# Order of the weight conversions in the opening of an FFT-and-MLP kernel: a skew of one piece, fold sums copied later, conversions moved ahead of the main loop

## The chip, the cores and the metric

One core of a Trainium2 chip. The metric is the device time of one execution in microseconds (us).

## The reference, cut to what matters

```python
x = 8 x 3008 x 256                                 # float32
X = real(fft(fft(x, axis=1), axis=2))              # over 3008 = 47 * 64, then over 256
h = X.reshape(24064, 256) @ w_in                   # 256 -> 2048, weights in float64
g = h * clip(h + 3, 0, 6) / 6
out = g @ w_out                                    # 2048 -> 256
```

## The kernel before

The main loop runs 4 x 12 x 8 steps: `mlp1` makes two half products u and v on TensorE, VectorE and ScalarE make the gated a, GpSimd adds up c, and `mlp2` accumulates seven products (acc). One step of it keeps TensorE busy for 4.75 us, and nothing else limits it. The *opening* must come first: stage 1 of the FFT for the first pair of batches (eight chunks, each a fold of x on VectorE and then matmuls), the conversion of 16 pieces of float64 weights to float32, the folding of w_in with the DFT matrix, and stage 2 of the first group.

A piece passes through three engines. `exponent_a` is two ScalarE instructions, `exponent_b` two matmuls, `exponent_c` one ScalarE instruction in place, `mantissa` two VectorE instructions, and `join` multiplies the two halves. After each second piece `use_pair` folds (w_in, on TensorE, with ScalarE copying the sums) or mixes (w_out, four VectorE instructions). Programs of the engines run in the order in which they are written.

```python
    ps_h = ctx.enter_context(tc.tile_pool(name="ps_h", bufs=3, space=PSUM))   # the three "uv" banks
    # ...
    def exponent_a(j):                                                       # ScalarE
        top = raw[j][:].bitcast(I16).rearrange("p (n four) -> p n four", four=4)[:, :, 3]
        for i in range(2):
            low = PM[:, j % 2, i].bitcast(U8).rearrange("p (n two) -> p n two", two=2)[:, :, 0]
            nc.scalar.activation(low, top, AF.Identity, bias=bias[:, i:i + 1], scale=(1 - 2 * i) / 16.0)

    def exponent_b(j):                                                       # TensorE, takes a uv bank
        ex = ps_h.tile([P, WB], F32, tag="uv", name="ex")
        for i in range(2):
            nc.tensor.matmul(ex[:], E[:, i], PM[:, j % 2, i].bitcast(F16), start=(i == 0), stop=(i == 1))
        exs[j] = ex

    def exponent_c(j):                                                       # ScalarE
        nc.scalar.activation(exs[j][:].bitcast(I32), exs[j][:], AF.Identity, scale=2.0 ** 23)
    # ... mantissa(j): two VectorE instructions; join(j): frac * ex on VectorE, frees the uv bank

    def fold_w_in(n):
        # ...
        for blk in range(2):
            ps = bank([P, WB], "wps")
            for i in range(2):
                nc.tensor.matmul(ps[:], C[:, i, blk * P:(blk + 1) * P], ws[i], start=(i == 0), stop=(i == 1))
            nc.scalar.copy(W1[:, blk, cs], ps[:])                            # at once
    # ...
    for c in range(NXC):                                                     # the eight chunks of stage 1
        if c + 2 < NXC:
            load_x(first, c + 2)
        load_w(c + 2)
        exponent_a(c)
        on_pe = c not in (2, 4, NXC - 1)          # fold_first: 3 VectorE instructions, more matmuls
        # ... fold of chunk c on VectorE
        if c > 0:
            join(c - 1)
        mantissa(c)
        for i in range(XC // 2):
            (stage1_first if on_pe else stage1)(first, c, i)
        exponent_b(c)
        exponent_c(c)
        if c in (2, 4, 6):
            use_pair(c // 2 - 1)
        # ...
    for j in range(NXC, 14):                                                 # the tail: pieces 8 to 13
        # ... load_w(j + 2)
        exponent_a(j)
        exponent_b(j)
        if j > NXC:
            exponent_c(j - 1)
        join(j - 1)
        mantissa(j)
        if j % 2 == 0:
            use_pair(j // 2 - 1)
    # ... last c, join and use_pair, then keep_awake(4)
    for i in range(2):
        stage2(first, 0, i)
    spread(first, 0)
    # ... pieces 14 and 15 are put behind steps 0 and 1 of the main loop
    mlp1(*chunk(0))                                                          # the fill of the main loop
    mlp1(*chunk(1))
    combine(*chunk(0))
```

`mlp1` takes two uv banks, u and v. `keep_awake(n)` issues n matmuls of zeros, meant to keep TensorE's clock up.

Of the kernel before, what the change touches and what calls it, by code (L numbers as in the profile page):

```python
# [56 lines left out]
def kernel(  # L57
# [171 lines left out]
    def evict_z(pr, c, i, ps):  # L229
        if i == 0:  # L230
            pr.z[c] = zpool.tile([PZ, XC, D], F32, tag="z", name="z")
            if c == 0:
                pr.zd = dpool.tile([2, NK1, 2, NS, D], F32, tag="zd", name="zd")
                pr.zq = dpool.tile([2, NK1, 2, NS], F32, tag="zq", name="zq")
# [13 lines left out]
    def turn_column(pr, c, z):  # L248
        n = XC if c < NXC - 1 else XC - 1
        zc = zpool.tile([PZ, XC], F32, tag="zc", name="zc")  # L250
        nc.scalar.activation(zc[:, 0:n], z[:, 0:n, P], AF.Identity, scale=F[0:PZ, 5 * PZ + NP * NXC:])
        to = pr.zq[:, :, :, c * XC:(c + 1) * XC].rearrange("b k c n -> c (b k) n")
        for ci in range(2):
            nc.sync.dma_start(out=to[1 - ci, :, 0:n], in_=zc[ci::2, 0:n])
        if n < XC:
            for ci in range(2):
                nc.sync.dma_start(out=to[ci, :, n], in_=z[ci::2, n, P])


    def load_g(pr, gr):  # L260
        g = gpool.tile([P, 2 * KK, D + 1], F32, tag="g", name="g")
        ks = slice(gr * 2 * KK, (gr + 1) * 2 * KK)
        for b in range(2):
            gb = g[b * N2:(b + 1) * N2]
            nc.sync.dma_start(out=gb[:, :, 0:D], in_=pr.zd[b].rearrange("k c n d -> (c n) k d")[:, ks, :])
            nc.sync.dma_start(out=gb[:, :, D], in_=pr.zq[b].rearrange("k c n -> (c n) k")[:, ks])
# [246 lines left out]
    def fold_w_in(n):  # L513

        cs = slice(n * WB, (n + 1) * WB)
        ws = [w.pop(("in", n, i)) for i in range(2)]
        for blk in range(2):
# [3 lines left out]
            nc.scalar.copy(W1[:, blk, cs], ps[:])  # L521
        nc.sync.dma_start(out=wn[n:n + 1], in_=W1[P - 1:P, 1, cs])
# [20 lines left out]
    nc.sync.dma_start(out=F[:], in_=c_stage1)  # L543
    nc.vector.tensor_copy(IX[:], F[:, 5 * PZ:5 * PZ + NP * NXC])
# [5 lines left out]
    load_t(0)  # L550

    load_forward(first, 0)
    load_forward(first, 1)
    load_partners(first, 0)
    load_w(0)
    load_partners(first, 1)
    load_w(1)

    bias = wpool.tile([P, 2], F32, tag="bias", name="bias")
    for i in range(2):  # L560
        nc.vector.memset(bias[:, i:i + 1], (2 * i - 1) * 7.5 / 16.0 - 896.0)
    nc.vector.memset(half[:], 0.5)
    PM = wpool.tile([P, 2, 2, WB], I16, tag="PM", name="PM")
    nc.vector.memset(PM[:], 0x6400)
    E = wpool.tile([P, 2, P], F16, tag="E", name="E")
    nc.scalar.copy(E[:], CE[:])
    for b in range(2):
        nc.vector.memset(T[(1 - b) * N2:(2 - b) * N2, b], 0.0)
    wn = dpool.tile([NWI, WB], F32, tag="wn", bufs=1, name="wn")

    for c in range(NXC):
# [3 lines left out]
        exponent_a(c)  # L575
        on_pe = c not in (2, 4, NXC - 1)
        if on_pe:
# [4 lines left out]
        if c > 0:  # L582
            join(c - 1)
        mantissa(c)
        for i in range(XC // 2):
            (stage1_first if on_pe else stage1)(first, c, i)
        exponent_b(c)
        exponent_c(c)
        if c in (2, 4, 6):
            use_pair(c // 2 - 1)  # L590
        if c in (3, 5):
            load_wn(PIECES[c - 3][1])
    load_g(first, 0)
    load_g(first, 1)
    load_t(1)
    for j in range(NXC, 14):
        if j + 2 < 16:
            load_w(j + 2)
        exponent_a(j)
        exponent_b(j)  # L600
        if j > NXC:
            exponent_c(j - 1)
        join(j - 1)
        mantissa(j)
        if j % 2 == 0:
            use_pair(j // 2 - 1)
    exponent_c(13)
    join(13)
    use_pair(6)
    load_wn(PIECES[6][1])  # L610
    load_wn(PIECES[8][1])
    keep_awake(4)
# [11 lines left out]
    def beside(p):  # L624
# [6 lines left out]
        if p == 0:  # L631
            for t, fs in enumerate([[(f, 14) for f in (exponent_a, exponent_b, mantissa)],
# [143 lines left out]
```

## Time and profile before

| | before |
|---|---|
| median of the first 3 runs | 2009.54 us (2009.37 to 2010.34) |
| profiled execution | 2007.46 us, span 2005.7 us |
| TensorE busy | 1962.5 us of the span |
| first matmul of acc | 95.78 us from the start |
| acc of the fifth step | 119.58 us |
| from there to the end | 1886.1 us |

The last row is the reason for looking at the opening alone. TensorE is full from the fifth step to its end, so a change of the opening is worth what it moves the acc of the fifth step.

ScalarE in the tail, from its timeline (columns: start, length, engine, line, operation with out<-in, and in brackets the idle time in front with what ended it):

```profile
62.40 0.59 ACT L521 COPY W<-wps 128x512 f32<-128x512 f32 x1 [2.18 <-PE wps L520]
64.12 0.58 ACT L521 COPY W<-wps 128x512 f32<-128x512 f32 x1 [1.13 <-PE wps L520]
...
71.50 0.58 ACT L521 COPY W<-wps 128x512 f32<-128x512 f32 x1 [3.21 <-PE wps L520]
```

The copies of the fold sums stand in ScalarE's order at the place where the fold's matmuls are only being issued, so ScalarE idles 2.18 and 1.13 us for one fold and 3.21 us ahead of the other's first copy, while the next pieces need it. The second is TensorE in the fill of the main loop:

```profile
91.15 1.10 PE L324 MATMUL v<-q,W 127*128 127x256 f32 x4 [1.64 <-DVE a L356]
...
94.84 1.10 PE L324 MATMUL v<-q,W 127*128 127x256 f32 x4 [1.72 <-DVE a L356]
95.78 0.60 PE L378 MATMUL acc<-a,G 128*128 128x256 f32 x2
```

With three uv banks, the v of the second and of the third step each wait for a bank: two holes of 1.64 and 1.72 us. Between them 2 us of matmuls run, and they run at full clock, 1.10 us for four of 256 columns.

### The profile page before, as it was taken

The page shows a single profiled execution, that of the slowest core. Times are in us where ns is not written, and L with a number is a line of the kernel's source. Part 1 is how long each engine was busy: PE and PEld are TensorE (multiplying, and loading weights), DVE is VectorE, ACT ScalarE, POOL GpSimd, SP SyncE. Part 2 cuts the span into 40 slices and gives each one's busy share as a digit, 9 for nine tenths or more (in the row PEclk, how much of TensorE's full clock was granted, in tenths as well). Part 3 has the DMA queues.
Part 4 walks back from the last instruction along what each step waited for, and adds up shares of the span by engine and source line. Part 5 has one row for each costly group of instructions (what it writes and reads, how often), then busy time and mean ns, then how long its engine had stood idle before and what let it go on. Part 6 is the DMA issues. An engine that isn't in the chain of part 4 may idle for free.

```text
span 2005.7 us, 28349 instructions
## 1 busy us (share of the span) xinstructions
PE 1962.5 (98%) x9144; PEld 1686.7 (84%) x9144; DVE 1444.6 (72%) x2707; ACT 694.7 (35%) x1196; POOL 1419.3 (71%) x1612
## 2 busy tenths in 40 slices
PE   8799999999999999999999999999999999999997
PEld 4388888888888888888888888888888888888886
DVE  6677767776777676777777777777678777777775
ACT  5433333333333333333333333333333333333322
POOL 3277778786677787777658877778666667667665
PEclk8899999999999999999999999999999999999999
DMA  9502211111111122210111221112110101101100
GB/s 294 143 21 56 59 39 47 49 47 35 27 35 50 40 49 53 54 51 25 41 26 29 67 55 42 51 43 52 35 27 19 27 17 26 33 12 27 27 12 19
DMA packets 159560, 93.52 MB, mean 47 GB/s; under 512 B 131595, under 2 KB 144395, under 8 KB 159414
## 3 DMA queue, kind: packets, MB, share of 16 engines
q1 hardware_dynamic: 149942, 58.23, 11.6%
q0 software_dynamic: 9472, 33.49, 6.0%
q8 instruction: 74, 1.21, 0.3%
q14 instruction: 72, 0.59, 0.1%
HBM read 54.32 MB, written 37.33 MB: 46 GB/s over the span
## 4 chain that ended last, share of the span: by engine, by line
PE 92%; DVE 3%; ACT 1%; issue 1%; POOL 0%; SPq 0%; DMA 0%; DVEq 0%; POOLq 0%; ACTq 0%
PE acc L378 55%; PE v L324 16%; PE u L324 16%; PE ps L279 2%; PE ps L226 2%; DVE a L356 1%; ACT t L353 1%; DVE u L337 1%; DVE s L329 1%; PE wps L520 0%; ACT PM L456 0%; DVE o L404 0%; DVE v L343 0%; PE awake L537 0%; PE ps L223 0%
## 5 line engine op out<-in xcount | busy, mean ns | idle before, releaser
L368 POOL TENSOR_TENSOR c<-a 128x512 f32<-128x512 f32 (+1 forms) x384 | 478.9, 1247 | 446.4 <-PE acc L378 361.3
L378 PE MATMUL acc<-c,G 128*128 128x256 f32 (+1 forms) x3072 | 712.1, 375 | 0.0
L353 ACT ACTIVATE t<-u,half 128x512 f32<-128x512 f32 (+2 forms) x416 | 272.3, 654 | 1101.1 <-DVE u L337 1089.5
L378 PEld LDWEIGHTS acc<-c,G 128*128 128x128 f32 x3072 | 577.5, 190 | 72.7
L329 DVE SCALAR_TENSOR_TENSOR s<-qn,WN,u 128x256 f32<-128x256 f32 x768 | 334.5, 477 | 351.6 <-PE u L324 348.8
L378 PE MATMUL acc<-a,G 128*128 128x256 f32 (+1 forms) x2304 | 550.6, 374 | 0.0
L378 PEld LDWEIGHTS acc<-a,G 128*128 128x128 f32 x2304 | 433.8, 190 | 57.4
L324 PE MATMUL v<-q,W 127*128 127x256 f32 x1536 | 397.0, 380 | 8.0 <-DVE a L356 8.0
L324 PE MATMUL u<-q,W 128*128 128x256 f32 x1536 | 394.3, 379 | 0.0
L324 PEld LDWEIGHTS v<-q,W 127*128 127x128 f32 x1536 | 289.5, 190 | 55.7 <-PE u L324 8.4
L324 PEld LDWEIGHTS u<-q,W 128*128 128x128 f32 x1536 | 287.3, 190 | 57.8 <-issue 13.9
L356 DVE SCALAR_TENSOR_TENSOR a<-t,u 128x512 f32<-128x512 f32 (+2 forms) x416 | 266.2, 646 | 95.2 <-ACT t L353 90.5
L368 POOL TENSOR_TENSOR c<-c,a 128x256 f32<-128x256 f32 (+1 forms) x384 | 275.2, 717 | 30.1
L368 POOL TENSOR_TENSOR c<-a,c 128x256 f32<-128x256 f32 (+1 forms) x384 | 275.0, 716 | 30.1
L337 DVE TENSOR_TENSOR u<-s,v 128x512 f32<-128x512 f32 (+1 forms) x384 | 263.0, 685 | 41.1 <-DVE s L329 1.4
L353 ACT ACTIVATE t<-v,half 128x512 f32<-128x512 f32 (+1 forms) x384 | 257.0, 669 | 5.8 <-DVE v L343 4.3
L343 DVE TENSOR_TENSOR v<-v,s 128x512 f32<-128x512 f32 (+1 forms) x384 | 257.7, 671 | 1.1
L356 DVE SCALAR_TENSOR_TENSOR a<-t,v 128x512 f32<-128x512 f32 (+1 forms) x416 | 255.2, 620 | 0.4 <-ACT t L353 0.2
L368 POOL TENSOR_TENSOR r<-w,e 128x256 f32<-128x256 f32 (+1 forms) x96 | 92.2, 981 | 3.8
L384 ACT ACTIVATE e<-acc 128x512 f32<-128x512 f32 (+1 forms) x192 | 86.9, 542 | 2.9 <-PE acc L378 2.8
L404 DVE STREAM_TRANSPOSE o<-r 128x256 f32<-128x256 f32 (+1 forms) x192 | 72.4, 414 | 6.4 <-POOL r L368 6.4
L236 ACT COPY z<-ps 96x512 f32<-96x512 f32 x64 | 36.9, 581 | 82.4 <-PE ps L226 64.1
(81 smaller groups left out, 750.2 us busy)
## 6 DMA issues: line engine op xcount, KB each, us to landing
out_dram<-o SPq DMA_DIRECT2D x736, 32.0 KB
zd<-z SPq DMA_DIRECT2D x32, 384.0 KB
g<-zd SPq DMA_DIRECT2D x48, 256.0 KB
xt<-in_x_dram POOLq DMA_DIRECT2D x21, 384.0 KB, 3.8
qn<-qd SPq DMA_DIRECT2D x23, 256.0 KB
st<-in_moe_w_in_dram POOLq DMA_DIRECT2D x8, 512.0 KB, 9.6
st<-in_moe_w_out_dram POOLq DMA_DIRECT2D x8, 512.0 KB, 5.2
xt<-in_x_dram POOLq DMA_DIRECT2D x7, 376.0 KB, 3.9
```

The lines of the kernel that those rows point to most:

```text
L226: nc.tensor.matmul(ps[0:PZ], F[0:PR, 0:PZ], y[:, 2 * i:2 * i + 2, :], start=True, stop=True)
L279: nc.tensor.matmul(ps[:, blk, 2 * u:2 * u + 2], g[:, kk, blk * (P + 1):blk * (P + 1) + P], T[:, :, gr, blk, kk], start=True, stop=True)
L324: nc.tensor.matmul(ps[:, i], W1[r, blk, f * P:(f + 1) * P], q[r, blk, of:of + KC], start=True, stop=True)
L329: nc.vector.scalar_tensor_tensor(s[:, i].rearrange("p k n -> p (k n)"), qn[:, of * N2:(of + KC) * N2], WN[:, f:f + 1], u[:, i].rearrange(" ...
L337: nc.vector.tensor_tensor(u[:, :, 0:ns], s[:, :, 0:ns], v[:, :, 0:ns], op=AL.add)
L343: nc.vector.tensor_tensor(v[:, :, 0:nm], v[:, :, 0:nm], s[:, :, 0:nm], op=AL.subtract)
L353: nc.scalar.activation(t, h, AF.Relu, bias=half[:], scale=scale)
L356: nc.vector.scalar_tensor_tensor(dst, t, 1.0, h, op0=AL.min, op1=AL.mult)
L368: nc.gpsimd.tensor_tensor(out, in0, in1, op=AL.add)
L378: nc.tensor.matmul(ch.acc[i // 2][:, i % 2, 0:ch.n], G[:, i, fc, :], mv, start=(fc == 0 and i % 2 == 0), stop=(fc == NF - 1), skip_group_c ...
L384: nc.scalar.mul(ch.e[:, k:i + 1, 0:ch.n], ch.acc[i // 2][:, 0:i + 1 - k, 0:ch.n], 1.0 / WS)
L404: nc.vector.transpose(o[:, 0:n // DH, h], ch.r[:, m, h, 0:n].rearrange("p (j i) -> p j i", i=DH))
```

## The change

Its intent: a piece's last steps (c, join, use of the pair) are written behind the next piece's first ones, so that no engine waits for a neighbour's latest result; the copies of the fold sums are put one piece later; pieces 14 and 15 are converted ahead of the main loop instead of within its first steps. Beside these, the front is reordered (x of chunk 0 first, T's zeros from ScalarE, the fill of PM as 32-bit words), chunks 2 and 4 take the TensorE form of the fold, and some small DMAs are merged.

```diff
     def evict_z(pr, c, i, ps):
         if i == 0:
-            pr.z[c] = zpool.tile([PZ, XC, D], F32, tag="z", name="z")
+            pool, tag = (gpool, "g") if pr.p == 0 and c % 3 == 2 else (zpool, "z")
+            pr.z[c] = pool.tile([PZ, XC, D], F32, tag=tag, name="z")
... turn_column and load_g: four zc buffers, fewer and larger DMAs
     def fold_w_in(n):
+        sums = []
         for blk in range(2):
             ps = bank([P, WB], "wps")
             ...
-            nc.scalar.copy(W1[:, blk, cs], ps[:])
-        nc.sync.dma_start(out=wn[n:n + 1], in_=W1[P - 1:P, 1, cs])
+            sums.append(ps)
+        def copy():
+            for blk in range(2):
+                nc.scalar.copy(W1[:, blk, cs], sums[blk][:])
+            nc.sync.dma_start(out=wn[n:n + 1], in_=W1[P - 1:P, 1, cs])
+        copies.append(copy)
... front:
-    load_t(0)
-    load_forward(first, 0)
-    load_forward(first, 1)
-    load_partners(first, 0)
-    load_w(0)
-    load_partners(first, 1)
-    load_w(1)
     for b in range(2):
-        nc.vector.memset(T[(1 - b) * N2:(2 - b) * N2, b], 0.0)
+        r = slice((1 - b) * N2, (2 - b) * N2)
+        t = T[r, b].rearrange("p g a k n -> p g (a k n)")
+        nc.scalar.copy(t, Z[r].unsqueeze(1).to_broadcast([N2, NG, 2 * TB]))
+    load_forward(first, 0)
+    load_partners(first, 0)
+    load_w(0)
+    load_x(first, 1)
+    load_w(1)
+    pending, copies = [], []
+    def on_scalar(j):
+        for i in pending:
+            exponent_c(i)
+        if j is not None:
+            exponent_a(j)
+        while copies:
+            copies.pop(0)()
+    def on_vector(j):
+        if j is not None:
+            mantissa(j)
+        for i in pending:
+            join(i)
+    def on_tensor(j):
+        if j is not None:
+            exponent_b(j)
+        done = pending.pop() if pending else 0
+        if done % 2:
+            use_pair(done // 2)
+        if j is not None:
+            pending.append(j)
     for c in range(NXC):
         ...
-        on_pe = c not in (2, 4, NXC - 1)
-        ... (the calls shown above)
+        if c < NXC - 1:
+            fold_first(first, c)
+        else: ...
+        on_scalar(c)
+        on_vector(c)
+        for i in range(XC // 2):
+            (stage1_first if c < NXC - 1 else stage1)(first, c, i)
+        on_tensor(c)
+        if c == 0:
+            load_t(0)
     load_g(first, 0)
-    for j in range(NXC, 14):
-        ... (the calls shown above)
-    keep_awake(4)
+    for j in range(NXC, 15):
+        if j < 14:
+            load_w(j + 2)
+        on_scalar(j)
+        on_vector(j)
+        keep_awake(1)
+        on_tensor(j)
+    ...
+    keep_awake(2)
     for i in range(2):
         stage2(first, 0, i)
     spread(first, 0)
... behind the steps: exponents, mantissas, joins of 14 and 15 and use_pair(7) are replaced by
+            for f in (on_scalar, on_vector, on_tensor):
+                after.setdefault(1, []).append((f, (None,)))
... fill:
+    on_scalar(15)
+    on_vector(15)
     mlp1(*chunk(0))
     mlp1(*chunk(1))
+    on_tensor(15)
     combine(*chunk(0))
```

## The prediction

> **What bounds the kernel now.** I read the page first, then engine time by stretches, the chain of waits in order of time, and the timelines of TensorE, ScalarE and VectorE over the first 140 us. From the page:
>
> ```profile
> PE 1962.5 (98%) x9144; PEld 1686.7 (84%) x9144; DVE 1444.6 (72%) x2707; ACT 694.7 (35%) x1196; POOL 1419.3 (71%) x1612
> PE   8799999999999999999999999999999999999997
> ```
>
> TensorE is the bound, and only the opening is not full. The engine time by stretches (columns: stretch, length, busy of PE, PEld, DVE, ACT, POOL, granted clock, DMA share, GB/s):
>
> ```profile
> 10.00:20.00 10.00, 6.41 (x15) 4.27 (x16) 6.03 (x9) 2.00 (x3) 4.20 (x6) 0.68 1.02 282
> 40.00:50.00 10.00, 10.00 (x41) 6.45 (x40) 5.98 (x15) 6.96 (x14) 1.06 (x2) 1.00 1.02 352
> 50.00:60.00 10.00, 5.54 (x19) 3.12 (x17) 6.69 (x18) 5.89 (x12) 1.45 (x2) 0.83 0.58 157
> 70.00:80.00 10.00, 6.31 (x13) 2.24 (x12) 4.11 (x11) 6.98 (x12) 1.50 (x2) 0.84 0.80 200
> 160.00:200.00 40.00, 40.00 (x187) 34.39 (x186) 28.57 (x52) 13.90 (x24) 30.44 (x35) 1.00 0.19 47
> ```
>
> To 50 us the DMA engines are full (share 1.02). From 50 to 80 us neither they nor TensorE are. From 160 us on TensorE is full; the change touches nothing there but some small DMAs. So the question is how much earlier TensorE reaches its steady step. In the timeline of TensorE that step is 4.75 us (the acc matmuls start at 119.58, 124.33 and 129.09), and 119.58, the fifth step's, is the first without a hole: my yardstick. The marks before it, from the timelines of TensorE and VectorE:
>
> ```profile
> 53.77 1.13 PE L226 MATMUL ps<-y,F 94*96 94x512 f32 x2 [3.09 <-DVE y L173]
> 60.27 0.38 PE L461 MATMUL ex<-PM,E 128*128 128x512 f16 x1 [0.28 <-ACT PM L456]
> 60.49 3.59 PE L520 MATMUL wps<-wi,C 128*128 128x512 f32 x8
> 68.08 5.29 PE L520 MATMUL wps<-wi,C 128*128 128x512 f32 x8
> 84.08 1.95 PE L279 MATMUL ps<-T,g 128*128 128x128 f32 x16
> 47.83 0.75 DVE L489 TENSOR_TENSOR G<-top,ex 128x256 f32<-128x256 f32 x2 [3.86 <-ACT ex L465]
> 112.15 1.12 DVE L508 TENSOR_TENSOR G<-G,b 128x256 f32<-128x256 f32 x1
> 118.64 1.10 PE L324 MATMUL v<-q,W 127*128 127x256 f32 x4 [0.89 <-DVE a L356]
> ```
>
> The last chunk of stage 1 waits 3.09 us for its fold, which stands in VectorE's order behind a join that idled 3.86 us for ScalarE. Six more weight pieces are converted until 79.5, then come awake matmuls, and stage 2 starts only at 84.08. Two more pieces (14, 15) are converted inside the first steps.
>
> **What the Trainium skill says.** "TensorE: Matmul & The Clock Gate", section "Part 1: The HAM clock gate": an idle window of about 3.4 us halves the clock. The trace agrees: eight wps matmuls take 3.59 us at full clock and 5.29 partly throttled, and after the hole from 9.6 to 13.6 us the slow spacing lasted until 23.8, longer than one window. The same page, "Architectural detail", calls ScalarE's and VectorE's queues strict FIFO; the trace agrees (fold 7 above). "SBUF — State Buffer", section "SBUF: two separate sides": VectorE with two SBUF inputs and GpSimd exclude each other. The trace agrees: this G subtraction has a mean of 0.42 us while GpSimd computes nothing, and took 1.12 at 112.15 beside GpSimd's adds.
>
> **The change part by part.**
>
> 1. *Front.* The 5.2 us of T memsets leave VectorE for ScalarE, idle until 13.75; x of chunk 1 and T no longer stand ahead of chunk 0's data. By the GB/s row, 0.38 + 0.26 MB at some 230 GB/s is 2.8 us, so fold 0 starts at about 9.5, not 12.24. This hardly counts by itself, since bytes bound what follows: the partner rows of chunk 7 were issued at 34.04 and took 12.1 us to land, 46.1, and the same bytes precede them still (estimate 45.5 to 46). It should keep the clock up: the hole after the first awake matmuls shrinks from 4 us to about 1.3.
>
> 2. *Stage 1.* Chunks 2 and 4 go to the TensorE form: 3.45 us instead of 1.9, TensorE +3.1; VectorE saves two operations of 0.6 in each. At full clock a chunk costs TensorE 3.45 + 0.43 (exponent), and after chunks 2 and 4 a w_in fold of 3.43. From chunk 2's data at 19.6: stage 1 of chunk 2 from 21 to 24.5; exponent and fold to 28.3; chunk 3 to 32.2; chunk 4 and fold to 39.5; chunk 5 to 43.4; chunk 6 to 47.3. VectorE: ScalarE's conversion for join 5 at 44.4, join and mix to 46.9 (0.75 + 1.7), fold 7's 2.47 us to its first usable y at 49.4. Stage 1 of chunk 7 is 2.15 us at full clock, to 51.7, and exponent 7 ends at 52.1, against 58.3: **6.2 us earlier**. The third z buffer and the four zc end ScalarE's waits on z stores (1.6 + 0.5 us between 20 and 53), part of this. Merged DMAs save issue on SP, which is not on this path.
>
> 3. *Tail of pieces, now 8 to 14 instead of 8 to 13.* ScalarE now runs c of the last piece, then a of the next: 0.5 + 1.4 us. But c must follow b on TensorE, which must follow a at once, so each piece gains a bubble of about 0.5 us: cadence 2.4, against 1.8 for the pairs at 75 to 79 us. Where a w_in fold follows, TensorE's order is fold 3.43, awake 0.86, exponent 0.43: 4.72. From the end of exponent 8 (52.1 + z copy and column 1.1, c 0.5, a 1.4 = 55.1): 4.72 + 2.4 + 4.72 + 3 x 2.4 = 19.0, so exponent 14 ends at 74.1. The old tail ended at 79.5 with one piece fewer, but it was throttled twice. Transfers keep up: each piece has three others ahead in its buffers, about 7 us, and lands in 5 to 6. Two awake (1.72) instead of four (4.9 as throttled): stage 2 starts at 75.9 instead of 84.24, **8.3 earlier**.
>
> 4. *Fill of the main loop.* ScalarE's c of 14 and VectorE's join of 14 now lie between the copy of qn and the first s. Before, s came 0.34 after the copy; now 0.5 + 0.7 + 0.1 = 1.3, a loss of 1.0. Stage 2 and spread (2.7) and the copy (0.6) put the first s at 80.5, not 87.89, 7.4 earlier. Exponent 15 then holds one of three uv banks from its matmul until its join after the second step. So u2 waits for u1's bank and the first acc matmuls start 8.7 after the first s instead of 7.9: 89.2, not 95.78. From there 4 steps of 4.75 and stage 2's 0.89 are 19.9, plus perhaps 0.9 for the join and mix of the last pair (3 us on VectorE beside GpSimd): acc of the fifth step at 110.0. Before, this stretch took 23.8, with exponents 14 and 15 inside. 119.58 - 110.0 = **9.5 us**.
>
> 5. *Clock.* The sum assumes full clock. Stretches with 1.3 us of matmul in 2.4 lie near where the window falls: before, about 1.5 in 3.4 was throttled. One slow window costs 1.5 to 2 us in a fold or the awakes; I take off 1.8.
>
> Sum: 9.5 - 1.8 = 7.7; 2009.5 - 7.7 = 2001.8 us.
>
> **Rivals.** (a) *The bubble eats the tail.* If the one-piece skew with nothing between a and c costs more than 0.5 each, or the clock stays down in it, the tail takes 24 to 26 us instead of 22 (52.1 to 74.1) and only 3 to 5 us remain: 2005. For it: ScalarE's chain is serial there. Against: an awake matmul in each round holds the clock. (b) *The front is throttled still.* If the new short hole lies on a window, chunks 1 and 2 run at half clock as before; with chunks 2 and 4 now heavier, chunk 7 comes 2.6 us later: 2004. (c) *DMA hides everything.* If chunk 7's data come at 48, only 2 us more are lost, since after 50 us the share is 0.58; it can't take back the gain of parts 3 and 4. (d) *All holes closed:* no slow window and chunk 7 unhindered: 10 to 11 us, 1999. (e) *The pinned uv bank* stalls more steps than one: 2 us lost; against it, VectorE needs about 3.7 us of each 4.75.
>
> **Range and chances.** My terms are worth +/- 2 us at the front, 2 in the tail, 1.5 in the fill; together about 3. So 1997.5 to 2006 holds it 8 times in 10. A change of 2% is 40 us, as much as nearly half the opening; the holes that can be closed add up to less. Faster by over 2%: 0.005; within 2%: 0.99; slower: 0.005.
>
> **What would show it.** Right: fold 0 near 9.5 us, no slow clock from 14 to 24 us; matmuls of chunk 7 near 49.5; exponent matmuls 2.4 us apart after 68 us; stage 2 near 76; first acc near 89 and the steady 4.75 us step from about 110; busy time from 160 us on unchanged. Wrong: stage 2 after 80 us, a granted clock under 0.8 in 55 to 80 us, a DMA wait ahead of the exponents of pieces 12 to 15, or a hole of over 2 us before the acc matmuls of steps two to four.

## The result, and the profile after

| | before | changed |
|---|---|---|
| median of 4 runs, same chip | 2009.45 us (2008.5 to 2010.34) | 2002.27 us (2001.0 to 2004.63) |
| ratio (95% interval) | | 0.9966 (0.9948 to 0.9983) |
| profiled execution | 2007.46 us, span 2005.7 | 2004.63 us, span 2002.9 |
| first acc | 95.78 | 93.67 |
| acc of the fifth step | 119.58 | 115.87 |
| from there to the end | 1886.1 | 1887.0 |

Ratios here and below are the mean time of one kernel's fast runs over that of the other's of the same rounds, so they are not quite the ratio of the medians quoted beside them. The change saves 7.2 us by the medians, 0.36%, and counts as the same within 2%. The predicted 2001.8 us lies 0.5 us under the median.

The two profiled executions happen to be badly matched: that of before was faster than all its timed runs, that of the changed kernel the slowest of its four. That is why both kernels were run again below (r1 and r5). The page of the changed kernel, first TensorE's line of the busy times, then its granted clock in 40 slices of the span:

```profile
PE 1965.6 (98%) x9178; PEld 1691.5 (84%) x9178; DVE 1437.2 (72%) x2701; ACT 701.2 (35%) x1198; POOL 1417.9 (71%) x1612
...
PEclk9899999999999999999999999999999999999998
```

TensorE is busy 3 us longer, not shorter: the time saved is idle time. A slice of the clock's line is 50 us; before, the first two slices stood at 8, now only the second does. The busy time by stretches of the changed kernel shows it more closely (columns as in the prediction: stretch, length, PE, PEld, DVE, ACT, POOL, granted clock, DMA share, GB/s):

```profile
10.00:20.00 10.00, 8.39 (x23) 5.47 (x24) 5.66 (x11) 4.31 (x8) 4.59 (x7) 0.66 1.03 256
...
80.00:90.00 10.00, 5.73 (x31) 4.09 (x29) 6.97 (x14) 5.88 (x10) 2.81 (x4) 0.89 0.14 44
90.00:100.00 10.00, 9.88 (x35) 8.37 (x36) 5.72 (x11) 1.29 (x2) 6.82 (x8) 0.77 0.27 79
...
160.00:200.00 40.00, 40.00 (x187) 34.39 (x186) 28.75 (x52) 14.14 (x24) 32.33 (x36) 1.00 0.17 44
```

From 160 us on TensorE is as full as before, as predicted. In the front TensorE is now 8.39 us busy of the ten, against 6.41, but the clock is no better there (0.66, before 0.68). And a new loss has come: from 80 to 100 us the clock is 0.89 and 0.77. A clock of half speed for a time t lowers the mean by t/2, so 0.11 and 0.23 of ten us are 2.2 and 4.6, together 6.8 us at half clock. The timeline of TensorE of the changed kernel shows where:

```profile
51.99 1.07 PE L226 MATMUL ps<-y,F 94*96 94x512 f32 x2 [2.77 <-DVE y L173]
...
57.90 3.59 PE L522 MATMUL wps<-wi,C 128*128 128x512 f32 x8
...
78.53 1.95 PE L280 MATMUL ps<-T,g 128*128 128x128 f32 x16
...
86.44 1.10 PE L325 MATMUL v<-q,W 127*128 127x256 f32 x4 [1.93 <-DVE a L357]
...
90.12 2.04 PE L325 MATMUL u<-q,W 128*128 128x256 f32 x4 [2.15 <-DVE a L357]
...
93.67 1.97 PE L379 MATMUL acc<-a,G 128*128 128x256 f32 x6
...
110.18 1.10 PE L325 MATMUL v<-q,W 127*128 127x256 f32 x4 [1.55 <-DVE a L357]
...
115.87 1.46 PE L379 MATMUL acc<-a,G 128*128 128x256 f32 x6
```

Chunk 7 starts 1.8 us earlier than before (51.99, 53.77), stage 2 5.6 us (78.53, 84.08), but the first acc only 2.1 us. The two holes of the fill are 1.93 and 2.15 us now, and from the second on the same four matmuls take 2.04 us instead of 1.10. Then, at 110.18, comes a third hole of 1.55 us. ScalarE of the changed kernel in the tail:

```profile
58.10 0.58 ACT L466 ACTIVATE ex<-ex 128x512 int32<-128x512 f32 x1 [0.46 <-PE ex L462]
...
59.90 0.58 ACT L527 COPY W<-wps 128x512 f32<-128x512 f32 x1
61.53 0.59 ACT L527 COPY W<-wps 128x512 f32<-128x512 f32 x1 [1.05 <-PE wps L522]
```

The first copy of a fold no longer waits (2.18 before), and the bubble of about 0.5 us of the skew is there: c waits 0.46 us for TensorE.

So the questions for the experiments were: which parts earn and which lose; is the half clock in the fill made by exponent 15's bank; why did chunk 7 come late; and how far can two single profiles be trusted.

### The profile page after: what moved, and what is told of

It is laid out like the page before. It is cut to its first block, busy times and chain, and to the rows that moved or that the text cites. A ratio compares the mean times of both kernels' runs of the same rounds, so it can differ in the third digit from the quotient of the medians.

```text
span 2002.9 us, 28366 instructions
## 1 busy us (share of the span) xinstructions
PE 1965.6 (98%) x9178; PEld 1691.5 (84%) x9178; DVE 1437.2 (72%) x2701; ACT 701.2 (35%) x1198; POOL 1417.9 (71%) x1612
## 4 chain that ended last, share of the span: by engine, by line
PE 93%; DVE 3%; ACT 1%; issue 0%; POOL 0%; DVEq 0%; POOLq 0%; ACTq 0%
PE acc L379 55%; PE v L325 16%; PE u L325 16%; PE ps L280 2%; PE ps L226 2%; DVE a L357 1%; ACT t L354 0%; DVE u L338 0%; DVE s L330 0%; ACT PM L457 0%; PE wps L522 0%; DVE o L405 0%; DVE v L344 0%; DVE u L341 0%; PE ps L223 0%
## 5 line engine op out<-in xcount | busy, mean ns | idle before, releaser
L369 POOL TENSOR_TENSOR c<-c,a 128x256 f32<-128x256 f32 (+1 forms) x384 | 274.7, 715 | 30.1
L369 POOL TENSOR_TENSOR c<-a,c 128x256 f32<-128x256 f32 (+1 forms) x384 | 274.6, 715 | 30.1
```

The lines of the kernel that those rows point to most:

```text
L369: nc.gpsimd.tensor_tensor(out, in0, in1, op=AL.add)
```

## The experiments

All kernels are the changed kernel with one edit, unless said otherwise; all gave correct results. Each was timed in five rounds beside before. The runs of one group of four share the runs of before: 2010.1 us median for r1 to r4, 2009.02 for r5 to r8, 2009.89 for r9 to r12. The three groups ran on three chips, so between groups the ratio to before is the safer comparison; 0.001 of it is 2 us. In all twelve profiles of the changed kernel and its variants the time from the acc of the fifth step to the end was 1886.4 to 1887.7 us, and in both of before 1886.1. So the mark decides, and it is given for each.

| run | edit | median us | ratio to before (95%) | chunk 7 | stage 2 | first acc | fifth step |
|---|---|---|---|---|---|---|---|
| before, first profile | | 2009.5 | | 53.77 | 84.08 | 95.78 | 119.58 |
| changed, first profile | | 2002.27 | 0.9966 (0.9948 to 0.9983) | 51.99 | 78.53 | 93.67 | 115.87 |
| r1 | none | 2003.8 | 0.9969 (0.9956 to 0.9983) | 50.23 | 76.28 | 92.10 | 114.83 |
| r2 | join ahead of mantissa | 2004.76 | 0.9975 (0.9962 to 0.9989) | 51.51 | 79.72 | 96.60 | 119.01 |
| r3 | a ahead of c in the tail | 2002.56 | 0.9967 (0.9953 to 0.9980) | 51.16 | 75.53 | 91.97 | 114.21 |
| r4 | exponent 15 behind the first acc | 2002.44 | 0.9965 (0.9952 to 0.9979) | 51.52 | 78.62 | 91.56 | 113.70 |
| r5 | before, unaltered | 2011.34 | 1.0010 (0.9996 to 1.0024) | 56.80 | 89.09 | 100.79 | 124.59 |
| r6 | awake matmuls in the fill | 2003.46 | 0.9973 (0.9959 to 0.9987) | 52.35 | 78.36 | 91.76 | 113.46 |
| r7 | last mix spread over four steps | 2005.58 | 0.9982 (0.9968 to 0.9996) | 54.17 | 80.17 | 95.31 | 116.13 |
| r8 | the front of before | 2006.67 | 0.9990 (0.9976 to 1.0003) | 54.27 | 80.29 | 95.43 | 118.12 |
| r9 | fold sums copied at once | 2008.28 | 0.9990 (0.9977 to 1.0004) | 50.72 | 79.87 | 95.02 | 117.72 |
| r10 | pieces 14 and 15 in the main loop | 1998.86 | 0.9943 (0.9929 to 0.9956) | 50.03 | 75.61 | 87.31 | 111.28 |
| r11 | chunks 2 and 4 in the VectorE form | 2005.24 | 0.9975 (0.9961 to 0.9988) | 58.92 | 86.84 | 101.98 | 124.54 |
| r12 | five edits together | 1997.66 | 0.9938 (0.9925 to 0.9952) | 48.46 | 64.33 | 83.05 | 103.39 |

The column of chunk 7 moves by several us between executions of code that is equal up to there (r1, r4, r6, r7). The marks after it are best read as differences along a row.

### r1: the changed kernel again

No edit. Theory: the half clock in the fill is a chance of where it falls. Rival: the code makes it.

> The changed kernel once more, unaltered, to see what of its first profile belongs to the kernel and what to one execution. If half-clock windows alone make its times spread from 2001.0 to 2004.6, a profile with fewer of them shows the first acc matmuls nearer to 91 than 93.67 us and a span of 1999 to 2000; time 0.3 to 0.4% under the kernel before. If the kernel itself always meets the half clock between 88 and 95 us, that stretch recurs in this profile too. If the DMA rate of 256 to 275 GB/s from 10 to 30 us was that execution's, it is 280 to 310 here and chunk 7 starts near 50 us instead of 51.99.

Measured: 2003.8 us, fifth step at 114.83. It recurs: the fill was at half clock for 10.2 us (clock 0.70 from 80 to 90 us and 0.79 from 90 to 100), and here from the first hole on, as TensorE's timeline of r1 shows:

```profile
84.19 2.04 PE L325 MATMUL v<-q,W 127*128 127x256 f32 x4 [1.93 <-DVE a L357]
```

In the front there is something to keep for r10, the first matmul of chunk 0 and the stretch around it in r1:

```profile
10.61 0.68 PE L199 MATMUL ps<-xt,F 94*96 94x258 f32 x2 [1.71 <-DVE xt L190]
...
10.00:20.00 10.00, 9.39 (x28) 6.29 (x29) 6.21 (x13) 4.89 (x9) 5.03 (x8) 0.66 1.03 277
```

The hole in front is only 1.71 us here, and the clock still fell to 0.66 in the stretch.

### r2: join ahead of mantissa

Theory: fold 7 comes late because mantissa 6 waits for its load (1.21 us in the changed kernel's VectorE timeline, at 46.06) with join 5 behind it. Rival: the wait merely moves.

```diff
     def on_vector(j):
+        for i in pending:
+            join(i)
         if j is not None:
             mantissa(j)
-        for i in pending:
-            join(i)
```

> VectorE does the join of the last piece before the mantissa of the next, instead of after it. Theory: chunk 7's fold came 2.4 us later than predicted because the mantissa of piece 6 waited for its load (until 46.06 us) and held join 5 and the mix behind it, and with them fold 7. Then with joins first, fold 7 starts by 47 to 48 instead of 49.4 and the kernel gains 1 to 2 us. Rival: chunk 6's own data came late (fold 6 at 43.48 after a DMA wait), so fold 7 is held by transfers whatever the order, and the gain is under 0.5 us.

Measured: 2004.76 us, no gain. VectorE's wait ahead of fold 7, first mantissa 6 in the changed kernel's first profile, then the join of piece 5 in r1 and in r2:

```profile
46.06 0.43 DVE L474 TENSOR_SCALAR top<-st 128x512 int32<-128x512 int32 x1 [1.21 <-DMA st<-in_moe_w_in_dram]
...
45.36 0.75 DVE L490 TENSOR_TENSOR G<-top,ex 128x256 f32<-128x256 f32 x2 [1.50 <-ACT ex L466]
...
45.58 0.75 DVE L490 TENSOR_TENSOR G<-top,ex 128x256 f32<-128x256 f32 x2 [2.50 <-ACT ex L466]
```

In r2 the join waits 2.50 us for ScalarE, and fold 7's part follows no sooner: its first y ran at 50.00, in the changed kernel at 50.48 and in r1, without the edit, at 48.73. So where the load comes in time, as in r1 and r2, the order gains nothing: mantissa 6, 1.1 us, now stands between the join and the mix. But mantissa 6 of r2 ran at 46.25 without a wait, so the theory for an execution with a late load was not put to the test, nor was the rival. That stays open.

### r3: a ahead of c in the tail

Theory: in the tail the bubble of half a us per piece is c waiting for b. With a of the next piece first it closes.

```diff
     def on_scalar(j):
+        if j is not None and j >= NXC:
+            exponent_a(j)
         for i in pending:
             exponent_c(i)
-        if j is not None:
+        if j is not None and j < NXC:
             exponent_a(j)
```

> In the tail alone (pieces 8 to 14), ScalarE does a of the new piece before c of the last, so that TensorE's b lies beside c. Theory: the bubble of 0.5 us a piece between a and c, as predicted, goes: cadence of the exponents without a fold falls from 2.37 to 1.9 us, and the whole tail from 18.9 to about 16.5; the kernel gains 2 to 2.5 us. Rival: c is late then, so join and fold of a pair come later and TensorE waits for them; the tail stays within 0.5 us of what it was.

Measured: 2002.56 us. From exponent 8 to exponent 14 it took 15.7 us (57.4 to 73.1), against 18.9 in both profiles of the changed kernel: the bubble is real. But 2.1 of the 3.2 us are given back before the first s, which comes 8.3 us after exponent 14 instead of 6.2. TensorE's timeline of r3:

```profile
81.71 1.10 PE L325 MATMUL u<-q,W 128*128 128x256 f32 x4 [1.61 <-DVE b L490]
```

The u of the second step waits 1.61 us for the join of piece 14, which a of 15 now precedes on ScalarE (0.31 in the changed kernel). The first acc is at 91.97, hardly ahead of r1. End to end the gain is about 1 us, within the noise; I had expected 2 to 2.5.

### r4: exponent 15 behind the first acc

Theory: exponent 15 holds one of the three uv banks from 87.4 us on, so that u of the third step waits too, and that joins the holes into one slow stretch. Behind the first acc it can't.

```diff
     mlp1(*chunk(0))
     mlp1(*chunk(1))
-    on_tensor(15)
     ...
+            after[0] = [(on_tensor, (15,))]
             for f in (on_scalar, on_vector, on_tensor):
                 after.setdefault(1, []).append((f, (None,)))
```

> The exponent matmul of piece 15 goes behind the first step's acc matmuls, where it takes a uv bank later. Theory: the held bank made u of step 2 wait 2.15 us, and without it u2 starts right after v1; the first acc matmuls come 0.8 us sooner after the first s (7.9 instead of 8.7 at full clock), and the hole no longer lets the clock drop between 88 and 95 us: gain 0.5 to 3 us. Rival: the wait comes back one or two steps later, when the same bank is held by piece 15 during u3 and v3: gain under 0.3 us.

Measured: 2002.44 us. From the first s to the first acc it took 8.28 us (83.28 to 91.56), where the changed kernel took 10.49 and 11.16. TensorE of r4 has this for the second hole:

```profile
90.63 1.10 PE L325 MATMUL v<-q,W 127*128 127x256 f32 x4 [0.61 <-DVE a L357]
```

u of the third step no longer waits at all and the v behind it 0.61 us; half clock lasted 3.4 us, not 6.8 or 10.2. The theory holds for the second hole and for the length of the slow stretch. It isn't the whole: the stretch began at the first hole here, as in r1, ahead of any exponent 15. In the changed kernel's first profile too the clock fell at 87.86 us (placed from stretches of 1 us), after the first hole and before the second opened at 87.97. Over the whole kernel the gain is 1 to 2 us by the mark, not resolved by the times.

### r5: before again

> The kernel before, unaltered, once more with a profile. Its first profile (span 2005.7, time 2007.46) was quicker than all its other runs (2008.3 to 2011.5), so the fifth step's start at 119.58 may be too early for the usual run. Expected: span near 2007.5 to 2009 and the fifth step's acc matmuls at 121 to 122 us, which with 114.8 to 115.9 in the changed kernel gives the measured 6 to 7 us. Rival: the first profile was typical up to 120 us and the missing 2 to 3 us lie elsewhere, later.

Measured: 2011.34 us, ratio 1.001 to before's other runs, so the same kernel. But its profile has the fifth step at 124.59, five us after that of the first profile, with chunk 7 at 56.8 and 13.7 us at half clock around it (53.8 to 67.4). I had expected 121 to 122. The lesson is about the yardstick: 119.58 was that of a fast execution. A run at before's median of 2009.5 has a span of 2007.7 us, as the time exceeds the span by 1.8 in the profiled run, and its fifth step at 2007.7 - 1886.1 = 121.6.

### r6: awake matmuls in the fill

Theory: the slow stretch in the fill is a matter of the clock alone; two matmuls in each hole keep it up.

```diff
+    def fill_awake(n):
+        ps = ps_d.tile([P, 2 * TB], F32, tag="d", name="awake2")
+        for i in range(n):
+            nc.tensor.matmul(ps[:], ones[:], W1[:, 0, 0:2 * TB], start=True, stop=True)
     ...
     mlp1(*chunk(0))
+    fill_awake(2)
     mlp1(*chunk(1))
     on_tensor(15)
+    fill_awake(2)
```

> The changed kernel with two awake matmuls (0.86 us each at full clock, result unused) between v0 and u1 and two more behind the exponent of piece 15, in the holes of the fill. Theory: the holes at v1 (1.93 us) and u2 (2.15) leave an idle window, which halves the clock for 7 to 10 us from about 86 us on in every profile so far; filled, the clock stays up, u2 and v2 take 0.86 each instead of 1.72, and from the first s to the first acc matmuls it is 8.7 to 9 us instead of 10.5 to 11.2: gain 2 to 3 us. Rival: the half clock comes from what precedes (the tail), not from the holes; then it recurs and the awakes only lengthen the fill: 0 to 2 us slower.

Measured: 2003.46 us. The stretches of r6 in the fill:

```profile
80.00:90.00 10.00, 8.81 (x38) 5.59 (x37) 7.14 (x14) 5.73 (x10) 2.97 (x4) 1.00 0.15 43
90.00:100.00 10.00, 10.00 (x47) 8.80 (x48) 7.76 (x15) 3.07 (x5) 6.91 (x9) 1.00 0.30 79
```

The clock never drops, and from the first s to the first acc it is 8.74 us (83.02 to 91.76). That is the 8.7 us that I had predicted: the term was right for full clock, and what lay over it in the changed kernel is the clock. The mark gains 1.4 to 2.4 us over the changed kernel's two profiles although chunk 7 came at 52.35; but the profiled run was the fastest of r6's five, and neither medians nor ratios show a gain.

### r7: the last mix spread over four steps

Theory: the third hole, 1.55 us at 110, comes from the join and mix of the last pair (4.9 us on VectorE beside GpSimd's adds). One mix instruction per step fits into each step's slack.

```diff
+    def mix_part(i):            # one of mix_w_out's four instructions, for n = 3
+        ...
-            for f in (on_scalar, on_vector, on_tensor):
+            for f in (on_scalar, on_vector):
                 after.setdefault(1, []).append((f, (None,)))
+            for i in range(4):
+                after.setdefault(1 + i, []).append((mix_part, (i,)))
```

> The four mix operations of the last w_out pair go one each behind the acc matmuls of steps 1 to 4 instead of all behind step 1. Theory: together (4.2 us beside GpSimd's adds) they hold VectorE so long that v of step 5 waits 1.55 us in every profile; spread, each about 1 us fits into the 1.1 us that VectorE has over in a 4.75 us step, and the stall goes: acc of the fourth step 5.6 us after the third's instead of 7.4, gain 1 to 1.6 us. Rival: spread, each takes the GpSimd lock at a bad time and two smaller stalls remain: gain under 0.5 us.

Measured: 2005.58 us. The hole is gone: from the third acc to the fourth it is 5.65 us (105.73 to 111.38), which is the step of 4.75 and stage 2's 0.9, where the changed kernel took 7.43. The time doesn't show it. In this profile chunk 7 came at 54.17 us, 2.2 to 3.9 us later than in those of the changed kernel, without any edit ahead of it; why the other four runs are no faster either (the ratio is 0.0013 above r1's, with overlapping intervals) stays open. VectorE of r7 has one odd line, the last mix instruction:

```profile
119.24 2.53 DVE L521 TENSOR_TENSOR G<-G,b 128x256 f32<-128x256 f32 x1
```

In other places this instruction takes 0.42 us. GpSimd computed without a pause from 117.6 to 121.5 us.

### r8: the front of before

Theory, my prediction's: the front hardly counts by itself. Rival: TensorE is the bound of stage 1, and what the front loses stays lost.

```diff
+    load_t(0)
     for b in range(2):
-        ... (nc.scalar.copy into T)
+        nc.vector.memset(T[(1 - b) * N2:(2 - b) * N2, b], 0.0)
     load_forward(first, 0)
+    load_forward(first, 1)
     load_partners(first, 0)
     load_w(0)
-    load_x(first, 1)
+    load_partners(first, 1)
     load_w(1)
     ...
-        if c == 0:
-            load_t(0)
```

> The changed kernel with the front of the kernel before: T zeroed by VectorE, T's first block and the x rows of chunk 1 loaded ahead of chunk 0's partners. Theory as predicted: bytes bound what follows, so fold 0 comes 2 to 3 us later (12.2) but chunk 7 starts within 1 us of the changed kernel's 50.2 to 52, and the time is 0 to 1 us longer. Rival: the clock hole after the first awake matmuls returns in full, chunks 1 and 2 run at half clock until 24 us with the heavier TensorE load, and chunk 7 and the end come 2.5 to 4 us later.

Measured: 2006.67 us, 2.9 us above r1's median and 4.4 above that of the first comparison (the intervals of the ratios overlap slightly). By the ratios it is 4.2 to 4.8 us. The fill of PM stays as in the changed kernel. TensorE of r8, the first matmul of stage 1:

```profile
13.85 1.17 PE L199 MATMUL ps<-xt,F 94*96 94x258 f32 x2 [5.03 <-DVE xt L190]
```

It waits 5.03 us (2.45 and 1.71 in the changed kernel), 10.2 us at half clock follow, and then TensorE is never idle: chunks 2, 3, 5 and 6 start at 25.8, 33.1, 44.3 and 48.2, where they started at 22.8, 30.1, 41.3 and 45.2 in the changed kernel. Three us late at the start of chunk 2, three us late at chunk 6; against r1 it is 4.0 at both, and 4.0 still at chunk 7. The rival holds: the front is worth 3 to 4 us by the marks of stage 1, and 4 to 5 by the ratios.

### r9: the fold sums copied at once

Theory: the deferred copies are what shortens the tail. Rival: ScalarE has time to wait.

```diff
-        copies.append(copy)
+        copy()
```

> The changed kernel with the two copies of each w_in fold's sums done at once behind the fold, as before, instead of behind the next piece's conversions. Theory: ScalarE then stands until the sums are there (about 2.2 us for the first and 1.1 for the second, as in the kernel before) with c and a of the next pieces behind it; in the tail each of the two folds costs 1.4 to 2 us more, in stage 1 part of it is hidden by transfers. The tail from exponent 8 to 14 grows from 18.9 to about 22 to 23 us; the kernel loses 3 to 4 us. Rival: ScalarE has the time over, since TensorE is busy with the fold anyway (4.7 us a round), and the loss is under 1 us.

Measured: 2008.28 us, 4.5 us above r1's median, 6.0 above the first comparison's. ScalarE of r9:

```profile
58.03 0.58 ACT L527 COPY W<-wps 128x512 f32<-128x512 f32 x1 [2.18 <-PE wps L522]
59.75 0.58 ACT L527 COPY W<-wps 128x512 f32<-128x512 f32 x1 [1.13 <-PE wps L522]
```

The waits of before are back, to the hundredth, and exponent 8 to 14 takes 22.0 us (56.3 to 78.3) instead of 18.9. That is 3.1 us in the tail, and the theory holds. The ratio to before is that of r8, 0.9990, which again makes 4.2 to 4.8 us, so which of the two gains is the larger can't be told. By the mark of this profile it is 1.9 to 2.9 us only, but that execution was among the faster ones of r9 (2006.12).

### r10: pieces 14 and 15 in the main loop again

Theory: converting the last pieces ahead earns what it says. Rival: it costs more in the fill than it saves in the steps.

```diff
-    for j in range(NXC, 15):
+    for j in range(NXC, 14):
     ...
+    for f in (on_scalar, on_vector, on_tensor):
+        f(None)
     ...
-            for f in (on_scalar, on_vector, on_tensor):
-                after.setdefault(1, []).append((f, (None,)))
+            for t, j in enumerate((14, 15, None)):
+                after.setdefault(t, []).extend((f, (j,)) for f in (on_scalar, on_vector, on_tensor))
     ...
-    on_scalar(15)
-    on_vector(15)
     mlp1(*chunk(0))
     mlp1(*chunk(1))
-    on_tensor(15)
```

> The changed kernel with pieces 14 and 15 converted within the first three steps of the main loop, as before, and the tail ending at piece 13. Theory: stage 2 starts about 1.5 to 2.4 us sooner (one round of 2.4 less, but the last c and join stand open), the first s comes 1.3 us sooner still, since no conversion stands ahead of it, and the fill has no held bank (7.9 us from s to acc instead of 10.5 to 11.2); but steps 0 to 4 take about 23.8 us instead of 22.2 to 22.7. Net: the move of these conversions is worth little or less than nothing, the kernel is 0 to 4 us FASTER than the changed one. Rival: as the change intends, conversions in the main loop cost TensorE more there than ahead of it; it is 1 to 4 us slower.

Measured: 1998.86 us (1996.57 to 1999.82). Each of its five runs is faster than each of the nine runs of the unaltered changed kernel (2001.0 to 2005.01). So this part of the change costs 4 to 5 us: 3.4 to 4.9 by the medians, 4.6 to 5.2 by the ratios, 3.5 to 4.6 by the mark. TensorE of r10:

```profile
10.97 0.68 PE L199 MATMUL ps<-xt,F 94*96 94x258 f32 x2 [1.71 <-DVE xt L190]
...
86.37 1.10 PE L325 MATMUL v<-q,W 127*128 127x256 f32 x4 [1.72 <-DVE a L357]
87.31 1.46 PE L379 MATMUL acc<-a,G 128*128 128x256 f32 x6
```

r1 makes a pair with it, as chunk 7 starts at 50.23 there and at 50.03 here. From the first s to the first acc r10 takes 7.9 us (79.42 to 87.31), as before did, at full clock; r1 took 11.2. From the first acc to the fifth step r10 takes 24.0, r1 22.7. So moving the two pieces ahead saves 1.2 us in the steps and loses 3.3 in the fill, beside 1.5 us by which the first s comes later. The 1.5 is too small, since r10 ran at half clock around chunk 7 (50.5 to 57.3 us) and r1 did not: counted from exponent 8, r1's first s comes 3.2 us later than r10's (25.1 against 21.9), which makes 3.2 + 3.3 - 1.2 = 5.3 us, near what the ratios say.

The first of those lines shows something else. The hole in front is 1.71 us, as in r1, to the hundredth. But the stretch from 10 to 20 us in r10:

```profile
10.00:20.00 10.00, 8.23 (x36) 5.44 (x36) 5.86 (x13) 5.84 (x10) 5.18 (x8) 1.00 1.04 269
```

Clock 1.00 here, 0.66 in r1, with the same code and the same hole. Stretches of 1 us place the falls and rises of the clock, and in all fourteen profiles those of one execution lie whole multiples of 3.41 us apart (in r1 the falls at 12.24 and 83.92, 21 of them). Carried back to the front, this grid holds r1's hole (8.90 to 10.61) inside one of its windows, 8.83 to 12.24, and the clock falls at the end of it; in r10, with a fall at 50.52, there is an edge at 9.56, within the hole (9.26 to 10.97). So where the window falls matters. It isn't the whole rule: in r10's fill the hole of 1.72 us (84.65 to 86.37) lies inside the window from 84.65 on, and the clock stays up.

### r11: chunks 2 and 4 in the VectorE form

```diff
-        if c < NXC - 1:
+        if c not in (2, 4, NXC - 1):
             fold_first(first, c)
     ...
-            (stage1_first if c < NXC - 1 else stage1)(first, c, i)
+            (stage1_first if c not in (2, 4, NXC - 1) else stage1)(first, c, i)
```

> The changed kernel with chunks 2 and 4 folded fully by VectorE, as before (TensorE 1.9 us instead of 3.45 for each, VectorE 1.2 us more). Theory: TensorE is the bound from chunk 2 to chunk 6 in the changed kernel (no hole between 20 and 48 us), so 3.1 us less of it brings chunk 6 up to 3 us sooner, but only to where its data are (about 41 to 43.5), and chunk 7 waits for VectorE's order as now: chunk 7 starts 0 to 1.5 us sooner and the time is the same within 1 us. Rival: VectorE gets behind, and fold 7 and chunk 7 come 1 to 3 us later.

Measured: four runs of 2003.68 to 2005.78 us and one of 2013.28, which was the profiled one. In that execution the DMA engines were full but moved only 233 GB/s from 10 to 20 us, and chunk 7 came at 58.92. The four others are a us or so above r1's median, which five runs cannot separate. What the form of chunks 2 and 4 is worth stays open; it is small.

### r12: five edits together

r3's order, r4's place of exponent 15, r7's spread mix, two awake matmuls in the first hole of the fill, and, beyond the single runs, stage 2 and spread of the first group in place of the awake matmuls of pieces 12 to 14.

```diff
-        keep_awake(1)
+        if j < 12:
+            keep_awake(1)
+        elif j < 14:
+            stage2(first, 0, j - 12)
+        else:
+            spread(first, 0)
         on_tensor(j)
     ...
-    keep_awake(2)
-    for i in range(2):
-        stage2(first, 0, i)
-    spread(first, 0)
... and the edits of r3, r4, r7 and the first half of r6's
```

> What the runs so far found, together: a before c in the tail (3.2 us shorter there), stage 2 and spread of the first group in place of the awake matmuls of pieces 12 to 14, exponent 15 behind the first acc, two awake matmuls between v0 and u1, and the last mix spread over four steps. Theory: the tail ends near 73 us, s starts 1.5 to 2.5 us after exponent 14 (76 instead of 81 to 83), the first acc 8 to 8.5 us later with the clock up (84 to 85, against 92 to 93.7), and the fifth step 20.7 after that: 105 instead of 115, so 6 to 10 us faster than the changed kernel, near 1994 to 1997. Rival: ScalarE, with three more copies in the tail, becomes its bound and the clock falls without the awakes; then 2 to 4 us faster only.

Measured: 1997.66 us (1992.81 to 1999.11), faster than both kernels: 12 us under before and some 5 to 6 under the changed one. It was profiled in its fastest execution, so 103.39 for the fifth step flatters it. From chunk 7 (48.46) to the first s it took 26.3 us, in r1 30.7; from there to the first acc 8.25; from the first acc to the fifth step 20.3, in r1 22.7. With only the first hole of the fill filled, the clock still fell for 3.4 us (78.4 to 81.8), after the next hole of 1.92 us, which ended at 78.05. The intervals of r10 and r12 overlap, so it isn't shown to be better than r10 with its one edit. r10's placing of pieces 14 and 15 together with r12's order of stage 2 was not tried.

## Why the prediction was right or wrong

The time, 2001.8 predicted and 2002.27 measured, was right, and so was the class. But the sum was right partly by luck, because two errors cancel. The table sets the prediction's chain of marks against the two profiles of the changed kernel (the exponents' ends are those of their matmuls):

| step | predicted | first profile | r1 |
|---|---|---|---|
| chunk 7 starts | 49.5 | 51.99 | 50.23 |
| to the end of exponent 7 | +2.6 | +3.7 | +2.8 |
| to exponent 8 | +3.0 | +2.4 | +2.8 |
| to exponent 14 | +19.0 | +18.9 | +18.9 |
| to stage 2 | +1.8 | +1.6 | +1.6 |
| to the first s | +4.6 | +4.65 | +4.65 |
| to the first acc | +8.7 | +10.5 | +11.2 |
| to the acc of the fifth step | +20.8 | +22.2 | +22.7 |
| sum | 110.0 | 115.87 | 114.83 |

The prediction took 1.8 us off the gain for the clock, so it stood for 111.8. The mean of the two profiles is 115.35: 3.5 us later than that. Against this, 119.58 for before was itself a fast execution's, and 121.6 belongs to the median, 2.0 later. Hence 121.6 - 115.35 = 6.2 us are left of the 7.7, and the times gave 6.2 (r1's ratio) to 7.2 (the medians). A yardstick from one profile carried as large an error as the chain.

Of the signs that I had named, fold 0 near 9.5, the exponents 2.4 us apart and stage 2 near 76 came (78.53, 76.28). "No slow clock from 14 to 24 us" and the first acc near 89 did not: half clock lasted until 19.6 and 19.1, and the first acc came at 93.67 and 92.10.

**Part 1, the front: a mechanism wrong in part.** Fold 0 started at 10.19 and 9.18, predicted 9.5. What failed is the sentence "This hardly counts by itself, since bytes bound what follows". r8 shows 3 to 4 us: TensorE is never idle from chunk 2 to chunk 6, so a later start isn't absorbed. My own part 2 laid out TensorE without a gap from 21 to 47.3 us, which contradicts part 1; I didn't set the two side by side. An earlier TensorE is absorbed, though, and there bytes do bound: r10 had no half clock in front, but its folds 1 and 2 waited 1.99 and 1.43 us for their data and its mantissa 6 0.72 us for its load, and chunk 7 came only 0.2 us ahead of r1's. And "It should keep the clock up" held by chance only: half clock was 6.8 us in r1 and nil in r10, after the same hole of 1.71 us.

**Part 2, stage 1: order right, 0.7 to 2.5 us late.** The chain said that chunk 7 stands behind join and mix on VectorE, and it does: 2.77 and 2.02 us of idle TensorE, ended by its y. What held that chain differed by execution. In the first profile the data were late: chunk 6's fold waited for its DMA until 43.48 and mantissa 6 for its load until 46.06. In r1, where fold 6 ran at 40.76, and in r8 join 5 waited for ScalarE behind TensorE's exponent 5, until 45.36 and 49.40. The rate from 20 to 30 us was 275 GB/s in the first profile and 301 in r1; in r11's slow execution it was 252 and chunk 7 came at 58.92. That the rate sets chunk 7 in the late cases was seen, not set, by an experiment, and r2 does not test it, since its load was in time.

**Part 3, the tail: right.** 19.0 predicted, 18.9 measured twice; r3 removes 3.2 us of it by reordering, and r9 shows that without the deferred copies it would be 22.0. Rival (a) thus didn't happen.

**Part 4, the fill: bank right, price too small.** The order of waits came out as told: join of 14 ahead of s (first s +4.65), and the held bank (8.74 in r6). The term of 8.7 was right at full clock. But the join of 14 holds up u of the second step (0.31 us) and lengthens the first hole from 1.64 to 1.93 us, and the bank of 15 moves u of the third step from between the two holes to behind them. TensorE then fell to half clock in the fill, for 6.8 to 10.2 us in all eight profiles that have this fill (the changed kernel, r1, r2, r7, r8, r9, r11, and r3 with ScalarE's order turned), and in none of the three with before's (before, r5, r10). The fall came in the first hole or before the second opened in the changed kernel, r1, r2, r3 and r4, and inside the second in r7, r8, r9 and r11; so the first hole can be enough, and the bank of 15 adds to the length. r6, which fills both holes, ends it; r4, which frees the bank, shortens it to 3.4 us. So the term "8.7 after the first s" measured 10.5 and 11.2. The last pair's "0.9 for the join and mix" was 1.8 in r7's comparison (7.43 - 5.65), since the mix took 4.2 us beside GpSimd, not the 3 for both.

**Part 5, the clock: size right, place wrong.** I took off 1.8 us for a slow window in the folds or awakes of the tail. The loss in the fill alone is 1.8 to 2.5 us (10.5 and 11.2 against 8.7), and the tail was clean in both profiles beyond exponent 8.

**What the parts are worth.** By the ratios of the runs that undo them, deferred copies and front are worth 4 to 5 us each, and moving pieces 14 and 15 ahead takes back about 5. That adds up to some 4 us of the 6 to 7; the rest, of the skew and the smaller edits, was not measured apart. The moved pieces are where a larger gain went. I had counted that part on the credit side without comparing it to leaving the pieces where they were: before paid 23.8 us from the first acc to the fifth step with both pieces inside, 3 us more than my 20.8 without them, and that was all there was to be had.

## What to carry to other kernels

Move work ahead of a loop only after pricing both places: within the first steps of this loop two pieces cost 1 to 2 us, ahead of it they cost 5 to 6. A buffer that is held across a fill can do harm twice, by the wait and then by the clock, when it takes away the work that stood between two short holes: half clock lasted 3.4 us without it (r4) and 6.8 to 10.2 us with it. And take a yardstick mark from a run near the median, or from several profiles, before working out a difference of a few us.

## What the Trainium skill lacked or had wrong

- "TensorE: Matmul & The Clock Gate", section "Part 1: The HAM clock gate": the table gives one or more idle windows (about 3.4 us) for the fall and one or more busy windows for the return. The grid of 3.41 us in r10 and r1 agrees with this length. But in the front and the fill of the changed kernel no hole was as long as a window. In the fill half clock followed a first hole of 1.93 us alone (first profile and r1), and in the front one hole of 1.71 us (r1, though not r10, which agrees with the page where it calls the window free-running). The page's "A second HAM failure mode: psum-queue depth-cycling" tells of short idle times that make the clock oscillate, but gives no length. And with TensorE working without a pause the return took two or three windows: half clock lasted 6.8 us in the front of the changed kernel and 10.2 us in that of before. A share of work in the window below which the clock falls would be needed; these runs show only that 1.64 and 1.72 us with 2 us of matmuls between them (before, r10) did no harm.
- "DMA: Bandwidth & Descriptors", section "Bandwidth": the rates are given by size, and by whether the other core of the pair streams too, which is not recorded here. With the engines at full share (1.02 to 1.04) the rate from 10 to 20 us was 282 GB/s in before, 256 and 277 in two executions of the changed kernel, and 233 in r11, and chunk 7 started anywhere from 48.5 us (r12, 280 GB/s) to 58.9 (r11). No page that I found says that it differs from one execution to the next.
- "SBUF — State Buffer", section "SBUF: two separate sides": that VectorE and GpSimd exclude each other is right, but not what it costs beside a chain of GpSimd instructions. A VectorE subtraction of 0.42 us took 2.53 us in r7, ending only after GpSimd had gone through two operations of 1.26 us and one of 0.22, where the page speaks of one instruction held out by one.
